# Attention with pooled keys plus a two-expert adapter on one core: the first batch's patch rows summed on two engines, and the second query group cast and transposed by DMA

## The chip, the cores and the metric

The kernel runs on one core of one Trainium2 chip. A core has five engines, each with its own instruction queue that is worked off strictly in order: TensorE (PE) multiplies matrices and, with an identity matrix, transposes them; VectorE (DVE) and ScalarE (ACT) do elementwise work; GpSimd (POOL) does elementwise work and issues the transfers that convert a type; SyncE (SP) issues transfers only. Sixteen DMA engines move the data. The metric is the device time of one execution in microseconds (us), smaller being better.

## The reference

For each of four batches there are 12288 queries of 128 numbers and an image of 384 x 32 positions of 128 numbers. The image is averaged over patches of 4 x 4, which leaves 768 rows, and multiplied by a matrix; the result serves as keys and values:

```python
kv_pool = kv.reshape(B, H // r, r, W // r, r, C).mean(axis=(2, 4))   # r = 4
kv_flat = kv_pool.reshape(B, -1, C) @ w_sr
s = scale * (q @ k.transpose(0, 2, 1))
a = np.exp(s); a /= a.sum(-1, keepdims=True) + 1e-09
x = a @ v
```

On x (49152 rows) stands a small mixture of adapters: logits = x @ w_gate for eight experts, the two best chosen, their softmax weights w, and out = x + sum of w * ((x @ A[e]) @ B[e]) with rank 16. All inputs and the output are float32.

## The kernel before

The 49152 queries are worked off in 96 chunks of 512, named k = 0 to 95; 24 chunks are one batch. Four chunks are a group of 2048 queries; group g holds chunks 4g to 4g + 3. A chunk goes through `scores` (six matrix products in three pairs, each pair into one of two PSUM buffers `sg`, each followed by one exponential on ACT into `em`), `attend` (24 matrix products into the single PSUM buffer `acc`, which also gives the row sums and the gate logits), `normalize` (DVE, `rinv` and `xn`; it frees `acc`), `top` and `route` (the choice of experts), `transposes`, `down`, `gate`, `up` and `finish` (the adapter). The loop over k from 4 to 95 staggers these steps over the chunks; every instruction is held in program order on its engine by `keep`, so what stands behind a waiting instruction waits with it.

**The prologue** makes what the loop needs: keys `kfT` and values `vx` of batch 0, and the scores of chunks 0 to 3. The image of batch 0 comes in three thirds h; a third has four patch rows r, and each row comes in two halves x, so SP issues 24 loads of 256 KB (`load_kv`, L98) in the order h, r, x. `prepare(0, nc.vector)` gives, for each third, the additions, then `keys(h)`, `keys2(h)` and `values(h)`. In the kernel before an addition (`pair_step`, L175) sums two of the four rows, rows 0 and 1 or rows 2 and 3, for one half: four additions on DVE for a third. `keys` then transposes on PE what is left, two row sums times two halves times four columns, which are 16 transposes of 128 x 128 float32 into one PSUM tile `kpT_ps`, where PE adds them up. The later batches are summed by POOL in the loop (L169, L171), from k = 10 on.

**The queries.** Matrix products need the queries transposed in bfloat16, `qT`. Groups 2 to 23 get there by two transfers: `cast_q(g)` (L79, issued by POOL) writes a bfloat16 copy of the group to a buffer in device memory, and `load_qT(g)` (L84, issued by SP) brings that copy in transposed. Groups 0 and 1 are loaded as float32 (`load_q`, L105) and turned by PE: `turn_q(g, m)` does four float32 transposes for chunk m of the group and a copy to bfloat16 on ACT (L116). Group 1's four loads stand behind the 24 image loads on SP; its four turns stand at the end of the prologue and in the steps k = 4, 5 and 6.

**The order around the change.** POOL's queue has nothing after the identity matrix but a one-element copy (`late`, L390), which waits for the last load of group 1 and so holds back the casts of groups 2 and 3 that stand behind it; the next entry is `route` of chunks 2 and 3. SP's queue has the image loads, group 1's loads, `b_f` and `a_f`, and then, in step k = 4, `load_qT(2)` and the first load of batch 1's image, one more of those in each of the next steps, and `load_qT(3)` at k = 8. PE's order at the seam is: scores of chunks 2 and 3 (last pair), the turn of chunk 4, `attend(0)`, then `scores(4, 0)`, and so on.

Of the kernel before, what the change touches and what calls it, by code (L numbers as in the profile page):

```python
# [15 lines left out]
ALU = mybir.AluOpType  # L16
# [4 lines left out]
def kernel(  # L21
# [10 lines left out]
    nc = tc.nc  # L32
# [7 lines left out]
    S = T // P  # L40
    GC = 4
# [35 lines left out]
    def cast_q(g):  # L77
        t = qdram.tile([GT, C], BF16, tag=f"q{g}", name=f"qbf{g}")
        keep(nc.gpsimd.dma_start(t, q[g // NG, (g % NG) * GT:(g % NG + 1) * GT]))  # L79
        q_bf[g] = t  # L80
# [20 lines left out]
    def load_q(g, lo, hi):  # L101
        if g not in q_f:
            q_f[g] = xpool.tile([P, GT // P, C], FP32, tag="xn", name="qf")
        src = q[0, g * GT:(g + 1) * GT].rearrange("(p j) c -> p j c", p=P)
        keep(nc.sync.dma_start(q_f[g][:, lo:hi], src[:, lo:hi]))  # L105

    def turn_q(g, m, engine):
        if m == 0:
            qT[g] = qpool.tile([P, GT], BF16, tag="qT", name="qT")
        ps = mtile([P, S, P], name="qT_ps")  # L110
        for i in range(S):
            mm(ps[:, i], q_f[g][:, m * S + i], id_f, is_transpose=True,
               start=(i == 0), stop=(i == S - 1))
        o = qT[g][:, m * T:(m + 1) * T].rearrange("p (s t) -> p s t", s=S)
        if engine is nc.scalar:
            keep(nc.scalar.copy(o, ps))  # L116
        else:
            keep(nc.vector.tensor_copy(o, ps))
# [7 lines left out]
    for h in range(3):  # L126
        for r in range(4):
            for x in range(2):
                load_kv(0, h, r, x)
    for m in range(GC):  # L130
        load_q(1, m * S, m * S + S)
    b_f = const.tile([P, C], FP32)
    keep(nc.sync.dma_start(b_f, moe_B.rearrange("e r c -> (e r) c")))
    a_f = const.tile([P, P], FP32)
# [23 lines left out]
    def prepare(b, adder):  # L158

        sums, rest = [], []  # L160

        def pool_step(h, step, lo, hi):
            t = kvr[b, h]
            if step < 3:
                u, v = t[:, 0].rearrange("p g c -> p (g c)"), t[:, step + 1].rearrange("p g c -> p (g c)")
            else:
                w = 2 * C if step == 3 else C
                u, v = t[:, 0, :, 0:w], t[:, 0, :, w:2 * w]
                keep(adder.tensor_tensor(u, u, v, op=ALU.add))  # L169
                return  # L170
            keep(adder.tensor_tensor(u[:, lo:hi], u[:, lo:hi], v[:, lo:hi], op=ALU.add))  # L171

        def pair_step(h, r, x):
            u, v = (kvr[b, h][:, r + i, x] for i in range(2))
            keep(adder.tensor_tensor(u, u, v, op=ALU.add))  # L175

        for h in range(3):
            if adder is nc.vector:
                sums.append([lambda h=h, r=r, x=x: pair_step(h, r, x)
                             for r in (0, 2) for x in range(2)])  # L180
                continue
            sums.append([lambda h=h, step=step, lo=lo: pool_step(h, step, lo, lo + 512)
                         for step in range(5) for lo in range(0, 1024 if step < 3 else 512, 512)])

        st = {}

        def keys(h):
            if h == 0:
                st["kpT"] = prep.tile([P, J, P], FP32, tag="kpT", name="kpT")
                kfT[b] = per_b.tile([P, J, P], BF16, tag="kfT", name="kfT")  # L190
            kpT = st["kpT"]
            ps = mtile([P, 2, P], name="kpT_ps")
            if adder is nc.vector:
                parts = [(r, i, c) for r in (0, 2) for i in range(2) for c in range(4)]
            else:
                parts = [(0, i, 0) for i in range(2)]
            for n, (r, i, c) in enumerate(parts):
                mm(ps[:, i], kvr[b, h][:, r, i, c * C:(c + 1) * C], id_f, is_transpose=True,
                   start=(n == 0), stop=(n == len(parts) - 1))
            keep(nc.vector.tensor_scalar(kpT[:, 2 * h:2 * h + 2], ps, 1.0 / 16.0, None,  # L200
                                         op0=ALU.mult))

        def keys2(h):
            kpT = st["kpT"]
            ps = mtile([P, 2, P], name="kfT_ps")
            mm(ps, w_sr_sb, kpT[:, 2 * h:2 * h + 2], start=True, stop=True)
            keep(nc.vector.tensor_copy(kfT[b][:, 2 * h:2 * h + 2], ps))

        def values(h):
            if h == 0:  # L210
                vx[b] = per_b.tile([P, J, VE], FP16, tag="vx", name="vx")
                keep(nc.vector.memset(vx[b][:, :, VC:VE], 1.0))
            ps = mtile([P, 2, VC], name="v_ps")
            for i in range(2):
                mm(ps[:, i], st["kpT"][:, 2 * h + i], wext, start=(i == 0), stop=(i == 1))
            keep(nc.vector.tensor_copy(vx[b][:, 2 * h:2 * h + 2, 0:VC], ps))
            if adder is not nc.vector:
                st["vb", h] = prep.tile([P, 2, C], BF16, tag="vb", name="vb")
                keep(nc.vector.tensor_copy(st["vb", h], ps[:, :, 0:C]))

        def turn(h):
            ps = mtile([P, 2, P], BF16, name="kfT_ps")
            for i in range(2):
                mm(ps[:, i], st["vb", h][:, i], id_bf, is_transpose=True,
                   start=(i == 0), stop=(i == 1))
            keep(nc.vector.tensor_copy(kfT[b][:, 2 * h:2 * h + 2], ps))

        for h in range(3):
            for f in (keys, keys2, values) if adder is nc.vector else (keys, values, turn):
                rest.append(lambda h=h, f=f: f(h))  # L230
        return sums, rest
# [155 lines left out]
    rest = []  # L387

    late = const.tile([P, 1], FP32)
    keep(nc.gpsimd.tensor_copy(late, q_f[1][:, GC * S - 1, 0:1]))  # L390
    for g in range(2, 4):
        cast_q(g)
    a_bf = const.tile([P, P], BF16)
    keep(nc.vector.tensor_scalar(a_bf, a_f, 0.5, None, op0=ALU.mult))
    b_bf = const.tile([P, C], BF16)
    keep(nc.vector.tensor_copy(b_bf, b_f))
    turn_q(1, 0, nc.scalar)


    att = {LA: [0], LA + 1: [1], LA + 2: [2, 3], LA + 3: [4, 5], LA + 4: [6, 7]}  # L400
# [16 lines left out]
    for k in range(LA, NCHUNK):  # L417
        b, i = divmod(k, NB)
        ka = att.get(k, [])
        kx = enter.get(k, [])  # L420
        if k % GC == 0:
            g = k // GC
            if 2 <= g + 1 < B * NG:
                load_qT(g + 1)
            if 4 <= g + 2 < B * NG and g + 2 not in q_bf:
                cast_q(g + 2)
        if b + 1 < B:
            if i == 4:
                sums, rest = prepare(b + 1, nc.gpsimd)
            if 4 <= i < 16:  # L430
                h, j = divmod(i - 4, 4)
                load_kv(b + 1, h, j, None)

        def after_norm(kn):
            top(kn)
            if kn == first[kn] + size[kn] - 1:
                route(first[kn])

        kn = [n for n in att.get(k - 1, []) if normed[n] == k]
        if k == LA:  # L440
            for s in range(S):
                attend(0, s)
            ka = []
        scores(k, 0)
        while later:
            later.pop(0)()
        for n in kn:
            normalize(n)
        pairs = [(kx[j] if j < len(kx) else None, kh[j] if j < len(kh) else None)
                 for j in range(max(len(kx), len(kh)))]  # L450
        for x_, h_ in pairs[:1]:
            transposes(x_, h_)
        if k + 1 in range(GC + 1, 2 * GC):
            turn_q(1, (k + 1) % GC, nc.scalar)
        scores(k, 1)
        for u_ in ku:
            up(u_)
            finish(u_)
        for a_ in ka[:-1]:
            for s in range(S):  # L460
                attend(a_, s)
            normalize(a_)
            after_norm(a_)
        if ka and len(ka) == 1:
            attend(ka[0], 0)
        for n in kn:
            after_norm(n)
        scores(k, 2)
        for x_ in kx[:1]:
            down(x_)  # L470
            gate(x_)
        if rest and i in (14, 15, 16, 18, 19, 20, 21, 22, 23):
            rest.pop(0)()
        for a_ in ka[-1:]:
            for s in range(1 if len(ka) == 1 else 0, S):
                attend(a_, s)
        for x_, h_ in pairs[1:]:
            transposes(x_, h_)
        for x_ in kx[1:]:
            down(x_)  # L480
            gate(x_)
        ku = kh
        kh = kx
        if b + 1 < B and 10 <= i < 21:
            h, j = divmod(i - 10, 4)
            for _ in range((4, 3, 1, 0)[j]):
                sums[h].pop(0)()
# [184 lines left out]
```

## Time and profile before

| what | value |
|---|---|
| median of three runs | 409.31 us (408.99 to 409.66) |
| the profiled execution's own time | 409.56 us |
| its span, first to last instruction | 407.6 us |
| PE busy | 379.6 us, 93% of the span |
| DVE, ACT, POOL busy | 324.5, 293.1, 170.7 us |
| mean granted TensorE clock | 0.991 |

The profile gives one execution. "Busy" counts an engine's instructions, and matrix products are pipelined, so a busy PE is not PE at its peak. A time such as 25.74 is in microseconds from the start of the span. In a row of the timeline the first number is the start, the second the duration, and `xN` says that N instructions of a kind were merged; a bracket at its end tells how long the engine sat idle before it and what ended that. For a transfer the row gives only its issue; the time to landing is in the answers for its line.

### The profile page before, as it was taken

To read this page: it belongs to the slowest core of one execution; us is meant where nothing else is said; L and a number is where in the kernel's file an instruction comes from. 1 tells how busy PE (TensorE), PEld (TensorE's weight loads), DVE (VectorE), ACT (ScalarE), POOL (GpSimd) and SP (SyncE) were. 2 spreads that over 40 slices of the span, in tenths; PEclk is the share of its full clock that TensorE was granted. 3 is DMA by queue.
4 is the path that set the end of the run, shared out by engine and by line. 5 is a ranking of instruction groups with operands and counts; after the bars stand their busy time and mean duration, and the time that the engine had idled before them with its cause. 6 is when DMAs were issued, how large, how long until landed. Compare 5 with 4: busy or idle time off the path is not lost.

```text
span 407.6 us, 11369 instructions
## 1 busy us (share of the span) xinstructions
PE 379.6 (93%) x4514; PEld 306.9 (75%) x4589; DVE 324.5 (80%) x948; ACT 293.1 (72%) x346; POOL 170.7 (42%) x289
## 2 busy tenths in 40 slices
PE   3798899999999999999999999999999999898992
PEld 2556778788888788888888788878888878677781
DVE  2553678888888888989888888988988888887873
ACT  2389468767678777867778877876777877665772
POOL 0010128888512319879411319879311322123342
PEclk9999999999999999999999999999999999999996
DMA  8998568984855999994855979996756548252213
GB/s 297 366 265 245 137 156 214 285 210 124 182 130 105 307 172 336 295 219 138 168 130 117 363 103 344 287 225 145 156 131 149 138 130 156 79 138 97 79 53 132
DMA packets 71319, 76.45 MB, mean 188 GB/s; under 512 B 49921, under 2 KB 50433, under 8 KB 70785
## 3 DMA queue, kind: packets, MB, share of 16 engines
q1 hardware_dynamic: 70128, 63.98, 53.8%
q0 software_dynamic: 704, 11.54, 16.7%
q8 instruction: 36, 0.59, 0.6%
q10 hardware_dynamic: 432, 0.20, 0.2%
q14 instruction: 19, 0.15, 0.1%
HBM read 50.53 MB, written 36.70 MB: 214 GB/s over the span
## 4 chain that ended last, share of the span: by engine, by line
PE 82%; DVE 7%; ACT 3%; DMA 3%; issue 2%; SPq 1%; POOL 1%; ACTq 0%; DVEq 0%; POOLq 0%
PE acc L68 34%; PE sg L68 23%; PE tt_ps L68 10%; PE h_ps L68 6%; PE d_ps L68 5%; ACT em L246 2%; DVE rinv L258 1%; DVE xn L263 1%; DMA kvr<-in_kv_dram 1%; SPq L98 1%; DMA w_sr_sb<-in_w_sr_dram 1%; PE kpT_ps L68 1%; DVE tts L333 1%; PE v_ps L68 1%; DVE hg L347 1%
## 5 line engine op out<-in xcount | busy, mean ns | idle before, releaser
L246 ACT ACTIVATE em<-sg 128x1024 f16<-128x1024 f32 x288 | 279.1, 1023 | 92.1 <-PE sg L68 59.5
L68 PE MATMUL acc<-vx,em 128*128 128x137 f16 x2280 | 171.7, 224 | 1.7 <-DVE xn L263 1.6
L68 PE MATMUL sg<-qT,kfT 128*128 128x512 bf16 x501 | 154.7, 378 | 2.7 <-ACT em L246 2.2
L68 PEld LDWEIGHTS <-em 128*128 128x128 f16 x2304 | 149.6, 98 | 4.0 <-DVE xn L263 2.2
L68 PEld LDWEIGHTS <-tts 128*128 128x128 bf16 x740 | 56.4, 98 | 45.8 <-DVE tts L333 2.1
L293 POOL TENSOR_TENSOR over<-xn,srt 128x128 f32<-128x128 f32 (+2 forms) x62 | 21.4, 365 | 157.0 <-DVE srt L281 157.0
L347 DVE TENSOR_TENSOR hg<-h_ps,gw 128x512 bf16<-128x512 f32 x93 | 64.2, 691 | 13.2 <-POOL gw L315 7.6
L263 DVE TENSOR_TENSOR xn<-acc,rinv 128x544 f32<-128x544 f32 x95 | 68.8, 725 | 3.3
L333 DVE COPY tts<-tt_ps 128x1024 bf16<-128x1024 bf16 (+1 forms) x96 | 64.4, 671 | 3.6 <-PE tt_ps L68 3.6
L171 POOL TENSOR_TENSOR kvr<-kvr 128x512 f32<-128x512 f32 x54 | 66.7, 1271 | 0.0
L360 DVE TENSOR_TENSOR osb<-d_ps,xn 128x512 f32<-128x512 f32 x91 | 62.6, 691 | 0.5 <-PE d_ps L68 0.5
L68 PEld LDWEIGHTS <-kfT 128*128 128x128 bf16 x576 | 45.9, 97 | 6.0 <-issue 3.7
L68 PEld LDWEIGHTS <-xn 128*128 128x128 bf16 x384 | 29.4, 98 | 22.0 <-ACT xn L585 0.5
L258 DVE RECIPROCAL rinv<-acc 128x4 f32<-128x4 f32 x95 | 17.3, 182 | 32.5 <-PE acc L68 31.4
L68 PE MATMUL h_ps<-a_bf,tts 128*128 128x128 bf16 x372 | 36.0, 219 | 2.8 <-DVE tts L333 1.6
L68 PE MATMUL tt_ps<-id_bf,xn 128*128 128x128 bf16 x372 | 35.9, 219 | 1.5
L68 PE MATMUL d_ps<-b_bf,tts 128*128 128x128 bf16 x364 | 35.2, 219 | 2.3 <-DVE tts L333 1.3
L68 PE MATMUL tt_ps<-id_bf,hg 128*128 128x128 bf16 x368 | 35.6, 219 | 0.3 <-DVE hg L347 0.3
L281 DVE MAX8 srt<-xn 128x8 f32<-128x8 f32 x380 | 34.3, 153 | 0.2
L314 POOL TENSOR_TENSOR gw<-th,over 128x128 f32<-128x128 f32 (+2 forms) x31 | 12.0, 389 | 39.2 <-ACT th L312 39.1
L68 PEld LDWEIGHTS <-hg 128*128 128x128 bf16 x384 | 25.5, 98 | 2.5 <-issue 1.1
L169 POOL TENSOR_TENSOR kvr<-kvr 128x512 f32<-128x512 f32 (+1 forms) x18 | 18.1, 1006 | 0.9
(77 smaller groups left out, 174.8 us busy)
## 6 DMA issues: line engine op xcount, KB each, us to landing
out_dram<-osb SPq DMA_DIRECT2D x95, 256.0 KB, 3.3
kvr<-in_kv_dram SPq DMA_DIRECT2D x36, 512.0 KB, 6.3
qbf<-in_q_dram POOLq DMA_DIRECT2D x22, 512.0 KB, 6.1
kvr<-in_kv_dram SPq DMA_DIRECT2D x24, 256.0 KB, 5.4
qf<-in_q_dram SPq DMA_DIRECT2D x1, 1024.0 KB, 5.1
qf<-in_q_dram SPq DMA_DIRECT2D x4, 256.0 KB, 5.2
qT<-qbf SPq DMA_TRANSPOSE x22, 6.3
out_dram<-osb ACTq DMA_DIRECT2D x1, 128.0 KB, 3.1
```

The costliest lines, as they stand in the source:

```text
L68: return keep(nc.tensor.matmul(*a, **k))
L169: keep(adder.tensor_tensor(u, u, v, op=ALU.add))
L171: keep(adder.tensor_tensor(u[:, lo:hi], u[:, lo:hi], v[:, lo:hi], op=ALU.add))
L246: keep(nc.scalar.activation(em[k][:, 2 * r:2 * r + 2], ps, AF.Exp, bias=0.0, scale=scale))
L258: keep(nc.vector.reciprocal(ri, acc[k][:, :, VC]))
L263: keep(nc.vector.tensor_tensor(x, acc[k][:, :, 0:VC], ri.unsqueeze(2).broadcast_to([P, S, VC]), op=ALU.mult))
L281: keep(nc.vector.max(srt[k0][:, m, s], xn[k][:, s, C:VC]))
L293: keep(eng.tensor_tensor(d, lg, so[:, :, i].unsqueeze(2).broadcast_to([P, n, 8]), op=ALU.subtract))
L314: keep(eng.tensor_tensor(w[:, 0:n], th, mask, op=ALU.mult))
L333: keep(nc.vector.tensor_copy(sb[:, lo:hi], ps[:, lo:hi]))
L347: keep(nc.vector.tensor_tensor(hg[k].rearrange("p s (e r) -> p (s e) r", e=E), hp[k].rearrange("p s (e r) -> p (s e) r", e=E), gw[k0][:, m ...
L360: keep(nc.vector.tensor_tensor(osb, dp[k], xn[k][:, :, 0:C], op=ALU.add))
```

## The change

The first part concerns the prologue's sums. For each third, rows 1, 2 and 3 are now added onto row 0, one after the other (`row_step`): the two additions of row 1 are done by POOL, the four of rows 2 and 3 by DVE. `keys` transposes only row 0's halves, eight transposes for a third in place of 16.

The second part concerns query group 1. Its four float32 loads, its four turns on PE and its four copies on ACT are gone. Group 1 is cast and brought in transposed as the later groups are: POOL casts groups 1, 2 and 3 one after the other, and SP issues `load_qT(1)` ahead of the loop. The one-element copy `late`, which the casts stand behind, now reads the last image load of batch 0.

```diff
-    for m in range(GC):
-        load_q(1, m * S, m * S + S)
...
-        def pair_step(h, r, x):
-            u, v = (kvr[b, h][:, r + i, x] for i in range(2))
-            keep(adder.tensor_tensor(u, u, v, op=ALU.add))
+        def row_step(h, r, x):
+            u, v = kvr[b, h][:, 0, x], kvr[b, h][:, r, x]
+            keep((nc.gpsimd if r == 1 else nc.vector).tensor_tensor(u, u, v, op=ALU.add))
...
-                sums.append([lambda h=h, r=r, x=x: pair_step(h, r, x)
-                             for r in (0, 2) for x in range(2)])
+                sums.append([lambda h=h, r=r, x=x: row_step(h, r, x)
+                             for r in (1, 2, 3) for x in range(2)])
...
-                parts = [(r, i, c) for r in (0, 2) for i in range(2) for c in range(4)]
+                parts = [(0, i, c) for i in range(2) for c in range(4)]
...
-    keep(nc.gpsimd.tensor_copy(late, q_f[1][:, GC * S - 1, 0:1]))
-    for g in range(2, 4):
+    keep(nc.gpsimd.tensor_copy(late, kvr[0, 2][:, 3, 1, 0:1]))
+    for g in range(1, 4):
         cast_q(g)
+        if g == 1:
+            load_qT(g)
...
-    turn_q(1, 0, nc.scalar)
...
-        if k + 1 in range(GC + 1, 2 * GC):
-            turn_q(1, (k + 1) % GC, nc.scalar)
```

## The prediction

> **What bounds the kernel now.** I read the page first, then the timeline of the first 62 us on all engines, then the answers for the lines of casts and transposing loads, and last the DMA queues in short stretches.
>
> ```profile
> PE 379.6 (93%) x4514; PEld 306.9 (75%) x4589; DVE 324.5 (80%) x948; ACT 293.1 (72%) x346; POOL 170.7 (42%) x289
> ...
> PE   3798899999999999999999999999999999898992
> ...
> PE 82%; DVE 7%; ACT 3%; DMA 3%; issue 2%; SPq 1%; POOL 1%; ACTq 0%; DVEq 0%; POOLq 0%
> ```
>
> A slice is 10.2 us. From the sixth on PE is nearly always busy, and 82% of the chain that ended last is PE. So from about 57 us on PE sets the pace, and what shifts PE's work before that shifts the end by the same amount. Both parts of the change lie before. This is the seam they touch, from the timeline:
>
> ```profile
> 23.24 0.42 PEld L68 LDWEIGHTS kpT_ps<-id_f,kvr 128*128 128x128 f32 x4 [0.18 <-DVE kvr L175]
> ...
> 25.74 0.19 POOL L390 COPY late<-qf 128x1 f32<-128x1 f32 x1 [24.44 <-DMA qf<-in_q_dram]
> 25.87 1.26 POOL L79 DMA_DIRECT2D qbf<-in_q_dram  x2
> ...
> 30.56 1.66 PE L68 MATMUL acc<-vx,em 128*128 128x137 f16 x24
> 31.33 0.63 ACT L116 CAST qT<-qT_ps 128x512 bf16<-128x512 f32 x1
> 31.36 2.52 SPq L84 DMA_TRANSPOSE qT<-qbf  x1
> ...
> 32.05 0.59 PE L68 MATMUL sg<-qT,kfT 128*128 128x512 bf16 x2
> ...
> 32.68 1.02 ACT L246 ACTIVATE em<-sg 128x1024 f16<-128x1024 f32 x1 [0.73 <-PE sg L68]
> ...
> 40.08 1.65 PE L68 MATMUL acc<-vx,em 128*128 128x137 f16 x24
> ```
>
> The reader is to see three times: chunk 4's first scores start at 32.05, right behind `attend(0)` (`acc` at 30.56); the two casts are issued at 25.87, once the last load of group 1 has landed; and the transposing load of group 2 is issued at 31.36, when its cast has landed. The third `acc` group, `attend(2)` at 40.08, is where I measure the shift.
>
> **Part one, the sums.** PE loses 24 of 48 transposes of `kpT_ps`. In the last third the weight loads of each four wait for a DVE addition (0.18 us in the row above); after the last addition four transposes remain, as now. So the saving is 0: the cover is DVE, whose additions per third stay four, 0.69 us each. POOL gets two per third, 1.26 to 1.28 us by L171's rows of the same shape. In the second third the image loads are issued 0.65 us apart and land 5.5 us later: row 1's halves at 14.7 and 15.3, the last half at 17.9. POOL adds until 16.0 and 17.25, so DVE's additions of the second half of row 2, then row 3, run from 17.3 to 19.25; before, the last ended at 18.7. That is 0.55 us late, and the last third follows with 0.55 us. `attend(0)` would start at 30.6, not 30.05 (where it could start once the turn ahead of it is gone). This costs 0 if chunk 4 waits for its queries beyond 32.2, and up to 0.55 us if not; that wait is the cover.
>
> No row of before shows POOL and DVE both adding float32 from SBUF; L171's additions run beside DVE work that reads at most one operand there. Bounds: side by side, as above; or in turns, 2 x 1.25 + 4 x 0.62 = 5.0 us a third, which is about 1 us late instead of 0.55, under the same cover. I take the first and keep the second.
>
> The Trainium skill speaks against this part: "SBUF — State Buffer", section Terms, says that GpSimd and VectorE take a shared port pair by an exclusive lock held for a whole instruction, the loser fully blocked. By that rule the sum takes the 1 us, still covered; no row here decides it.
>
> **Part two, the path of group 1's queries.** Removed: four SP issues (0.35 to 0.54 us each) and 1 MB of loads, which nothing waits for but `late`; four turns, 0.45 us of PE each; four copies on ACT, 0.47 us each in a row. Moved: `late` waits for the last image load, issued at 17.92 and landed 5.2 us later, at 23.1, and not for 25.69. Added: one cast, one transposing load, and PE's wait for that.
>
> 1. The first cast starts 0.18 us after that landing, as before: 23.28. Behind it on POOL stand the two other casts (0.5 to 0.76 us each), then nothing until 49.6.
> 2. The first cast before landed 5.5 us after its issue, and casts follow each other:
>
> ```profile
> L79 POOL DMA_DIRECT2D qbf<-in_q_dram x22: 512/579/755, 25.9 to 341.2; - x22
> ...
> DMA to landing us min/median/max: 5.4/6.1/8.9
> ```
>
> So `load_qT(1)` is issued at 23.28 + 5.47 + 0.02 = 28.77. The second cast landed 2.55 us after the first (31.34 and 33.89); its last packet left an engine at 33.48, 7.6 us after the first issue. A third adds 2.5 us: cast packets occupy the engines until 23.28 + 7.6 + 2.5 = 33.4.
> 3. The transposing load:
>
> ```profile
> L84 SPq DMA_TRANSPOSE qT<-qbf x22: 2289/3870/7020, 31.4 to 357.2; - x22
> ...
> DMA to landing us min/median/max: 4.7/6.3/9.5
> ```
>
> The first took 4.74 us. Its packets began at 32.96, when the engines had finished the second cast's, and it landed 2.6 us after the last cast packet. Do other packets get past a cast? The queues between 234.5 and 236.5, where a cast is in flight and a transposing load has just been issued:
>
> ```profile
> q0 software_dynamic: 3, 0.10, 29.5%
> q1 hardware_dynamic: 7, 0.02, 3.0%
> ...
> qT<-qbf SPq DMA_TRANSPOSE x1, 9.2
> ```
>
> In 2 us seven packets of the other queue start, and the load takes 9.2 us; its first packet starts at 239.0, as the last cast packet ends. A cast is 16 packets of 32 KB, one for each engine, 2.5 to 3.5 us each, and an engine takes nothing else meanwhile. After the change the third cast is queued on every engine before `load_qT(1)` is issued. Two ends: the load passes between the second and the third cast, 28.77 + 4.74 = 33.5; or it stands behind the third, 33.4 + 2.6 = 36.0. I take 36.0, by the 234 row.
>
> 4. PE's `scores(4, 0)` moves from 32.05 to 36.05, 4.0 us. Some comes back: from 32.68 on ACT was the pace (exponentials every 0.955 us, three copies of 0.47 us among them). Before, `attend(2)` followed the first exponential of chunk 4 by 7.4 us. After: four exponentials free the buffer for the third pair of chunk 5 (3.8), that pair (0.45), the rest of `attend(1)` (1.3), `rinv` and `xn` (1.0): 6.55 us, 0.85 less. Net: 4.0 - 0.85 = 3.15 us, and break-even where the queries land at 32.85.
>
> Behind `load_qT(1)` on SP wait `load_qT(2)`, four image loads of batch 1 and `load_qT(3)`. Pushed back some 3 us each they land near 39, 46 and 49; they are needed at 50.4 (chunk 8), 63.4 (POOL's first addition) and 65. The first output store, at 53.4, is behind them too. Cost 0, by 10 us of slack.
>
> Sum: 0 + 3.15 on the profiled execution's 409.56 gives 412.7; that execution is 0.25 above the median of the runs, which takes me to 412.5. The cases below are against that median, 409.31, too.
>
> One more cost has no row: PE would idle from about 32.1 to 36.05, and from 11 to 392 us its longest gap is 1.1 us at a granted clock of 1.00. Below, 0; above, half speed: PE's 4.1 us of work in chunks 4 and 5 (six pairs of 0.43 us, one `attend` of 1.5) doubled, against the 6.05 us that ACT's pace allows, 2.1 us more. I take 0, by the last stretch, where the clock stays at 0.99 between 396 and 400 with PE busy 2.36 of 4 us, and keep 2.1.
>
> The Trainium skill, "TensorE: Matmul & The Clock Gate", Part 1, says that an idle window of about 3.4 us halves PE's clock and that it takes as much sustained work to return; its windows run free, so a gap of 4 us may or may not hold one. By it the sum could be up to 2 us higher.
>
> **Rivals.**
> - B, the load passes the third cast. The queries land at 33.5 to 34.1, PE loses 0.7 to 1.2 us: 410.0 to 410.5. For it: the casts are separate packets with a gap between them; against: the next one started there within 0.02 us.
> - C, the held load plus one more loss (PE's clock, up to 2.1, or POOL's issue of the casts held up by DVE's additions until 25.0 (1.7)): up to 414.6. For it: the gap is new, and DVE adds from 21.9 to 24.9 without pause; against: no row shows either.
> - D, not slower: cast and transposing load are hidden. It decides at a landing of 32.85, which leaves 9.55 us from 23.28. The fastest cast and load of 22 each, 5.4 + 4.7, make 10.1. Landing by 32.1, where `attend(0)` ends with the later sums, gives 0.75 us back: 408.6.
>
> **How the numbers follow.** A measurement of this kernel can tell about 0.2% (0.8 us) from no change. A, as summed: 0.62; B: 0.17, a third of it within 0.2%; C: 0.14; D: 0.07, half of it faster by over 0.2%. Faster 0.03, same 0.10, slower 0.87. The range leaves out D, a little of B and the far end of C: 410.2 to 414.3.
>
> **What the profile will show.** Right: casts issued near 23.3, the transposing load's wait on SP ending near 28.8, PE idle before `sg` of chunk 4 until about 36 with the DMA as releaser, `attend(2)` near 43.2, the same rhythm after. Wrong: a landing near 33.5 (step 3), casts issued well after 23.3 (step 1), or a granted clock under 1 near 36 (the last cost).

## The result: 1.45% slower, nearly twice the loss that was forecast

The changed kernel takes 415.15 us (median of four runs, 414.99 to 415.64) against 409.28 us: a ratio of 1.0145, 95% interval 1.0127 to 1.0162. The direction was forecast; the time lies 2.65 us over the forecast and 0.85 us over the end of its range. The profiled execution took 415.29 us, with a span of 413.3 us.

The page of the changed kernel; as before, one slice is about 10.3 us, and PEclk gives the granted clock of PE in tenths:

```profile
PE   3784989999999999999999999999999999899992
...
PEclk9997999999999999999999999999999999999997
...
PE 82%; DMA 7%; DVE 4%; ACT 2%; SPq 1%; issue 1%; POOL 0%; DVEq 0%; ACTq 0%
```

PE still sets the pace from the sixth slice on. New are the dip in PE's row in the fourth slice, a clock of 0.7 in the same slice, and 7% of DMA in the chain where 3% stood before. Where that lies, the chain of the changed kernel shows in order of time (start, duration, what):

```profile
17.79 5.20 DMA kvr<-in_kv_dram
22.99 0.05 issue
23.04 0.12 POOL late L388
23.17 6.33 DMA qbf<-in_q_dram
29.50 0.02 issue
29.52 8.73 DMA qT<-qbf
38.25 0.05 issue
38.30 1.05 PE sg L68 x2
```

The last image load, the cast of group 1, its transposing load, and only then chunk 4's scores: three transfers in a row, the last two of them new on the chain. From the timeline of the changed kernel, with PE's wait in the bracket:

```profile
31.98 1.66 PE L68 MATMUL acc<-vx,em 128*128 128x137 f16 x24
...
38.30 1.89 PE L68 MATMUL sg<-qT,kfT 128*128 128x512 bf16 x4 [4.66 <-DMA qT<-qbf]
...
46.23 1.66 PE L68 MATMUL acc<-vx,em 128*128 128x137 f16 x24
```

Chunk 4's scores start at 38.30 and not 32.05, 6.25 us later; `attend(2)` starts at 46.23 and not 40.08, 6.15 us later. From there to the last chunk's exponentials the two traces stay 6.0 to 6.1 us apart, so the loss arises ahead of 47 us (the spans differ by 5.7 us; 0.3 us comes back behind those exponentials).

In stretches of the changed kernel (stretch, length, busy time of PE, weight loads, DVE, ACT and POOL, granted clock, DMA share, GB/s):

```profile
22.00:35.70 13.70, 9.70 (x66) 6.04 (x65) 7.16 (x23) 9.48 (x10) 2.20 (x5) 1.00 0.91 156
35.70:42.50 6.80, 3.82 (x8) 1.10 (x9) 0.09 (x1) 2.95 (x4) 0.00 (x0) 0.50 1.01 225
42.50:48.00 5.50, 5.43 (x62) 4.08 (x62) 1.69 (x6) 4.81 (x7) 0.00 (x0) 1.00 1.10 325
```

PE's clock is at half from 35.7 to 42.5; before, it was full throughout this time.

### The profile page after: what moved, and what is told of

Read it like the earlier page. It is cut to its first block, busy times and chain, and to the rows that moved or that the text cites. A ratio compares the mean times of both kernels' runs of the same rounds, so it can differ in the third digit from the quotient of the medians.

```text
span 413.3 us, 11370 instructions
## 1 busy us (share of the span) xinstructions
PE 383.7 (93%) x4549; PEld 304.4 (74%) x4549; DVE 325.4 (79%) x948; ACT 291.2 (70%) x342; POOL 178.4 (43%) x296
## 4 chain that ended last, share of the span: by engine, by line
PE 82%; DMA 7%; DVE 4%; ACT 2%; SPq 1%; issue 1%; POOL 0%; DVEq 0%; ACTq 0%
PE acc L68 34%; PE sg L68 28%; PE tt_ps L68 9%; PE h_ps L68 5%; PE d_ps L68 5%; DMA kvr<-in_kv_dram 3%; DMA qT<-qbf 2%; DMA qbf<-in_q_dram 2%; SPq L98 1%; DVE xn L261 1%; DMA w_sr_sb<-in_w_sr_dram 1%; PE v_ps L68 1%; DVE tts L331 1%; ACT em L244 1%; DVE hg L345 1%
## 5 line engine op out<-in xcount | busy, mean ns | idle before, releaser
L68 PE MATMUL sg<-qT,kfT 128*128 128x512 bf16 x576 | 173.7, 384 | 6.8 <-DMA qT<-qbf 4.7
L68 PE MATMUL tt_ps<-id_bf,hg 128*128 128x128 bf16 x368 | 35.6, 219 | 0.3 <-DVE hg L345 0.3
L312 POOL TENSOR_TENSOR gw<-th,over 128x128 f32<-128x128 f32 (+2 forms) x31 | 12.0, 387 | 38.9 <-ACT th L310 38.8
```

The costliest lines, as they stand in the source:

```text
L68: return keep(nc.tensor.matmul(*a, **k))
L312: keep(eng.tensor_tensor(w[:, 0:n], th, mask, op=ALU.mult))
```

## The experiments

**Is it the casts behind it that hold the load?** The casts of groups 2 and 3 wait on POOL, behind a one-element copy that reads group 1's transposed queries.

```diff
         if g == 1:
             load_qT(g)
+            late2 = const.tile([P, 1], BF16)
+            keep(nc.gpsimd.tensor_copy(late2, qT[1][:, GT - 1:GT]))
```

> The changed kernel, with the casts of groups 2 and 3 held on GpSimd until group 1's transposed queries have landed. Theory (the transposing load stands behind the third cast's 32 KB packets, and behind an instruction fetch on one DMA engine): with no cast behind the first, the queries land 4.7 to 5.3 us after the load's issue near 29, at 33.7 to 34.5 and not 38.25; PE's gap is under 1 us, its clock stays at 1.00 there, and the time is 410.0 to 411.0 us. Rival (the load is slow by itself, right behind the cast that wrote its source): landing still near 38, time near 415.

Measured: 411.16 us (ratio 1.0052, 1.0036 to 1.0069), 4.0 us less than the changed kernel. The answer for the transposing load of this run:

```profile
L84 SPq DMA_TRANSPOSE qT<-qbf x1: 2519/2519/2519, 28.8 to 28.8; - x1
...
DMA to landing us min/median/max: 4.7/4.7/4.7
```

4.7 us instead of 8.73; the queries land at 33.5. So the rival falls: the load isn't slow by itself, it stands behind the casts. The queues of the changed kernel from 30.5 to 32.4, with the load issued at 29.52, show the same from the other side; this is all that starts in these 1.9 us:

```profile
DMA packets 4, 0.07 MB, mean 34 GB/s; under 512 B 2, under 2 KB 2, under 8 KB 2
...
q0 software_dynamic: 4, 0.07, 17.7%
...
qT<-qbf SPq DMA_TRANSPOSE x1, 8.7
```

Not one packet of the load's queue (q1) is among them. The time is 0.16 us over what I expected. The profiled execution is the lowest of six (409.76 to 412.13), so its trace shows the landing, not the typical time. Two executions, at a mean granted clock of 0.992, took 409.76 and 410.07 us; the other four, at 0.977 to 0.986, took 411.03 to 412.13. There is no trace of those four, so whether the clock makes the difference is not shown, and what keeps this kernel 2.0 us above the kernel before stays open in part: the landing at 33.5, against the break-even at 32.85, accounts for 0.65.

**What does the half clock cost?** First in the changed kernel itself: PE gets work in its wait.

```diff
                 attend(0, s)
             ka = []
+            idle = mtile([P, T], name="idle_ps")
+            for _ in range(20):
+                mm(idle, kfT[0][:, 0], qT[0][:, 0:T], start=True, stop=True)
```

> The changed kernel, with 20 matrix products of 128 x 512, whose result nobody reads, on PE between the first chunk's attention and chunk 4's scores, about 4.3 us of work inside the 4.66 us that PE waits there. Theory (the wait lets PE's clock fall to half from 35.7 to 42.6, which costs 0.75 us of the 0.85 us that ACT should give back): the clock stays at 1.00, the queries land as before at about 38.2, and the time is 414.2 to 414.6 us. Rival (the clock's fall costs nothing, because ACT is the pace in that stretch): time 415.0 to 415.5.

Measured: 414.19 us (ratio 1.0123, 1.0108 to 1.0139), at the lower end of what the theory had, and the clock stays at 1.00 from 20.8 to 403 us. But in this run's trace the queries also land 0.9 us sooner, at 37.34, so it does not separate the two. A pair of runs does. The first takes the first part out (pairs on VectorE, 48 transposes) and holds the casts:

> Group 1 by DMA with the casts of groups 2 and 3 held until its queries have landed, and the patch rows summed in pairs by VectorE with 48 transposes, as in the kernel before. Theory (with the casts held, the queries land near 33.5; what the first part costs, 1.66 us alone, is then no longer covered, which is why holding the casts gave 411.16 and not 410): without the first part the loss is that of a landing at 33.5 against the break-even at 32.85, 0.7 us, so 409.6 to 410.4. Rival (the 2 us left are the DMA path's own): 410.8 to 411.5.

Measured: 412.74 us (1.0080, 1.0061 to 1.0099), well outside what I expected. The queries landed at 35.0 and not 33.5, and PE, whose prologue ends sooner without the first part, waited 3.0 us and lost its clock. The second adds 13 products in that wait, by the same edit as above:

> The run with held casts and sums in pairs, plus 13 matrix products of 128 x 512, whose result nobody reads, ahead of chunk 4's scores, 2.8 us of work in PE's gap from 32.0 to 35.0. Theory (that gap halves PE's clock from 34.0 to 40.8, which stretches the way from chunk 4's first scores to the third attention group from 7.2 to 8.5 us): the clock stays at 1.00, that way takes 7.2 us, and the time falls from 412.74 by 1.0 to 1.5, to 411.2 to 411.7 us. Rival (ACT is the pace in that stretch, and the clock costs nothing): 412.4 to 413.0.

Measured: 411.44 us (1.0059, 1.0040 to 1.0078), 1.30 us less (1.1 us if each is set against the runs of the kernel before that were taken with it), with the load landing at 35.0 in both. The stretch after the wait, first in the run without the 13 products:

```profile
34.10:40.80 6.70, 5.31 (x16) 2.04 (x17) 0.07 (x1) 4.33 (x5) 1.10 (x3) 0.50 0.89 168
```

and in the run with them:

```profile
34.10:40.80 6.70, 4.78 (x33) 2.41 (x33) 0.23 (x2) 5.09 (x7) 1.09 (x3) 1.00 0.88 171
```

From chunk 4's first scores to `attend(2)` it took 8.54 us at half clock and 7.21 us at full clock. The wait's clock is thus shown to cost 1.3 us here. In the changed kernel the same way took 7.93 us, which puts it at 0.7 us there. What is left of the second run, 2.15 us, is the landing: 35.0 against the break-even at 32.85.

**What does the first part cost alone, and why?**

```diff
-            u, v = (kvr[b, h][:, r + i, x] for i in range(2))
-            keep(adder.tensor_tensor(u, u, v, op=ALU.add))
+            u, v = kvr[b, h][:, 0, x], kvr[b, h][:, r, x]
+            keep((nc.gpsimd if r == 1 else nc.vector).tensor_tensor(u, u, v, op=ALU.add))
```

(with the eight transposes and the order of the changed kernel; group 1 loaded and turned by PE as before)

> The kernel before with the first part alone: patch rows summed by GpSimd and VectorE, 24 transposes in place of 48; query group 1 loaded and turned by PE as before. Prediction's step: the additions are 0.55 us late, or 1.0 us where VectorE and GpSimd take turns, no cover here: 409.8 to 410.3. Theory from the changed kernel's trace (PE, with less to do in the prologue, gets its full clock at 22.1 us and not at 10.8, and a VectorE addition took 1.74 us beside a GpSimd one): the first chunk's attention starts 1.4 to 1.9 us later, time 410.7 to 411.2. Rival (fewer transposes help): under 409.0.

Measured: 410.83 us (1.0038, 1.0023 to 1.0053), 1.66 us over the kernel before. Then the same with work for PE where it waits for the additions:

```diff
+            if adder is nc.vector:
+                idle = mtile([P, P], name="idle_ps")
+                for _ in range(8):
+                    mm(idle, id_f, id_f, is_transpose=True, start=True, stop=True)
             for n, (r, i, c) in enumerate(parts):
```

> The first part alone, with eight transposes of the identity matrix, whose result nobody reads, put ahead of each third's eight transposes on PE, where PE waits for the additions. Theory (of the 1.7 us that the first part costs alone, PE's half clock from 14.3 to 21.2 us is the larger share): the clock stays at 1.00 from about 11 us on and the time falls from 410.83 to 409.6 to 410.1 us; what is left is the later additions, 0.5 to 0.9 us. Rival (the additions, VectorE held up beside GpSimd, cost all of it): 410.6 to 411.2.

Measured: 409.89 us (1.0018, 1.0009 to 1.0027). The stretch from 14.3 to 21.1 us of the run without the added work, and then of the run with it:

```profile
14.30:21.10 6.80, 5.58 (x17) 2.81 (x18) 3.94 (x6) 1.94 (x2) 3.70 (x4) 0.50 1.03 379
```

```profile
14.30:21.10 6.80, 4.84 (x27) 2.95 (x28) 4.46 (x7) 2.53 (x3) 3.95 (x4) 1.00 1.05 402
```

The transposes that the first part saves had kept PE's clock up. Of 1.66 us, 0.94 go with the clock; the other 0.7 are put down to the later additions. The two traces place only a part of this: `attend(0)` starts at 31.60 and, with the added work, at 31.20 (30.56 before), which is 0.40 us for the clock and 0.64 us for the additions. Why these are late is in the answers for the additions' line of the changed kernel, on DVE and then on POOL (min, median, max in ns):

```profile
L173 DVE TENSOR_TENSOR kvr<-kvr x12: 677/680/1740, 9.7 to 25.6; 128x512 f32<-128x512 f32 x12
...
  POOL kvr L173: 2.0, 1
```

```profile
L173 POOL TENSOR_TENSOR kvr<-kvr x6: 1257/1264/1271, 8.4 to 21.1; 128x512 f32<-128x512 f32 x6
```

The DVE addition of 1740 ns starts at 9.72 while POOL adds from 9.65 to 10.92, and it ends 0.54 us after that one. The first part alone has two such, of 1703 and 1372 ns, and each of them, too, ends 0.55 us after the POOL addition beside it. In the run with the added work the second third has one of 1742 ns (from 15.78 us): that third's last addition ends at 19.33 and not 18.69, the last third's at 25.04 and not 24.40, 0.64 us late like `attend(0)`. DVE waits for POOL, as the Trainium skill has it ("SBUF — State Buffer", Terms).

**Does the second part alone explain the whole?** The kernel before with the second part only:

> The kernel before with the second part alone: query group 1 cast and transposed by DMA; patch rows summed in pairs by VectorE, 48 transposes on PE. Theory (the wait for the queries decides and covers the first part): the queries land at 36.5 to 38.3, time 413.5 to 415.3. Rival (the first part costs its 1.4 us on top): 411.5 to 413.5.

Measured: 415.24 us (1.0149, 1.0134 to 1.0164). It equals the changed kernel. So behind the wait for the queries the first part costs nothing on balance, as forecast, and nothing is gained by it. The two traces are not alike, though: without the first part the queries landed at 37.67, 0.58 us sooner, but PE waited 6.3 us, was at half clock from 33.4 to 43.6, and took 8.60 us from chunk 4's scores to `attend(2)` where the changed kernel took 7.93. In these two the differences nearly cancel.

**Why was the landing at 38.25?** The changed kernel once more, for a second trace:

> The changed kernel once more, for a second profile of it. Theory of the landing at 38.25 (15 of the load's 16 completions at 36.7, the last behind an instruction fetch on its DMA engine): cast issues near 23.2, most completions near 36 to 37, and a last one that is 1 us or more later only where an instruction fetch or a late cast stands on its engine. Rival (the last completion is always late): the same 1.5 us without a fetch near it. Time 415.0 to 415.6.

Measured: 416.88 us in a single run, 1.3 us over the range I gave, with the queries landing at 39.02. Here all 16 completions are late (15 of them from 38.9 to 39.0), not one, so the theory as I wrote it fits the first trace only. What this trace shows is a stop in the middle of the load. The queues from 34.6 to 38.0, in 40 slices of 0.085 us:

```profile
GB/s 18 105 205 289 289 289 476 271 271 271 274 256 27 18 15 0 0 0 0 0 6 9 9 9 9 9 12 9 9 130 289 289 289 289 292 342 271 271 280 289
...
q8 instruction: 1, 0.02, 2.1%
```

For 1.4 us, from 35.6 to 37.0, nearly nothing moves on any engine, and the one transfer besides is a 16 KB instruction fetch from 35.16 to 36.33. In the first trace such a fetch lies from 36.01 to 37.18, with 15 completions at 36.6 to 36.7 and the last at 38.25. Between the last cast packet and the landing lie 3.8 and 4.5 us in these two traces and 3.8 in the run with 20 products, all three with a 16 KB fetch in that time. It is 2.6 us in the kernel before, with no fetch; 3.0 with the first part alone, where a 16 KB fetch ends 0.25 us into that time; and 3.1 with the second part alone, where a fetch of 8 KB lies in it (36.08 to 36.49). That the fetch is the cause is argued from these six traces; I did not move a fetch to try it.

**Do the traces point to a faster kernel?** Two places in the kernel before have an engine that waits beside one that is the pace. In the last third DVE's four additions start late; and ACT copies group 1's turned queries while it is the pace and DVE idles.

```diff
-            keep(adder.tensor_tensor(u, u, v, op=ALU.add))
+            eng = nc.gpsimd if (h, r) == (2, 0) else adder
+            keep(eng.tensor_tensor(u, u, v, op=ALU.add))
```

> The kernel before with one edit: in the last third GpSimd sums rows 0 and 1, in pairs as before, and VectorE only rows 2 and 3; the 48 transposes on PE stay. Theory (before, VectorE's four additions of the last third start at 21.9 us, behind other work, and end 0.6 us after the last image load could have let them): the last addition ends at 23.8 and not at 24.4, everything up to the first chunk's attention moves 0.5 to 0.6 us ahead, time 408.5 to 408.8. Rival (the queue of exponentials on ACT takes the gain): 409.0 to 409.3.

Measured: 408.33 us (0.9981, 0.9972 to 0.9990), 0.17 us under what I expected. The last addition ends 0.78 us after the last image load's landing, where it ended 1.3 us after it before. In this trace `attend(2)` starts at 39.76, 0.32 us sooner than before, so the theory places less than half of the 0.83 us gained.

```diff
-    turn_q(1, 0, nc.scalar)
+    turn_q(1, 0, nc.vector)
...
-            turn_q(1, (k + 1) % GC, nc.scalar)
+            turn_q(1, (k + 1) % GC, nc.vector)
```

> The kernel before with one edit: the four copies of group 1's turned queries are made by VectorE and not by ACT. Theory (from 32.7 to 41 us ACT is the pace, with three of these copies among its exponentials, while VectorE idles 4 us): the third group of attention products starts 0.8 to 1.4 us sooner, time 407.8 to 408.5. Rival (VectorE's chain from normalization to routing is the pace there): 409.0 to 409.4.

Measured: 407.89 us (0.9970, 0.9959 to 0.9982), the fastest of all. ACT and PE in this run:

```profile
32.23 4.69 ACT L246 ACTIVATE em<-sg 128x1024 f16<-128x1024 f32 x5 [1.21 <-PE sg L68]
...
39.13 1.65 PE L68 MATMUL acc<-vx,em 128*128 128x137 f16 x24
```

Five exponentials now run in a row, with no copy among them. From `attend(0)` to `attend(2)` it takes 9.0 us instead of 9.5; the rest of the 1.27 us this trace does not place (its image loads landed 0.5 us sooner).

> The two edits together: GpSimd sums rows 0 and 1 of the last third, VectorE makes the four copies of group 1's queries. If both theories hold and add up, 407.2 to 408.0 us; if one of them takes the other's gain, 408.2 to 408.7.

Measured: 408.20 us (0.9973, 0.9964 to 0.9983). In time the two do not add up. In the traces they do, up to the last two exponentials, which start at 390.43 before and at 389.97, 389.49 and 389.00 in the three runs; why the times do not follow is not shown. The intervals of the three overlap, so which is the best of them is not settled.

## Why the prediction was wrong

**What bounds, and part one: right.** PE sets the pace behind the seam, the transposes saved gain nothing, and the wait for the queries covers what the first part costs: the second part alone gives the same time as both. Without that cover the forecast's 0.55 to 1.0 us was too little; it is 1.66 us, because the step looked for the saved transposes' worth only in PE's time and not in PE's clock (0.94 us).

**Steps 1 and 3, the mechanism: right.** The casts were issued at 23.17 (forecast 23.28), the load stood behind the third cast and not between the casts, and with the casts held its time to landing is 4.7 us, as step 3 had it from the row before. The first cast took 6.33 us to land and not 5.47, which cost nothing while the load had the third cast to wait for.

**Steps 2 and 3, the size: wrong by 2.25 us.** The landing was set at 36.0 and came at 38.25. Two terms were too small. Step 2 let the cast packets end at 33.4; the last ended at 34.45, because one of the 16 cast packets of each round ended 0.9, 1.0 and 1.3 us behind the next-latest one (0.3 us in both rounds of the trace before). What makes that packet late is not shown. Step 3 let the load land 2.6 us after that; it took 3.8, for which the instruction fetch is argued and not shown. Both numbers were read from one instance in the trace before, as if they were fixed.

**The last cost, PE's clock: wrong by 0.75 us.** It was named and bounded (0 to 2.1 us), and set at 0 by a stretch where PE was busy in short bursts. That was a misreading. The answer from which the stretch was taken has one more row, and in it the clock is at half (kernel before):

```profile
396.00:400.00 4.00, 2.36 (x24) 1.51 (x25) 2.57 (x6) 2.62 (x8) 1.73 (x3) 0.99 0.02 4
400.00:407.60 7.60, 1.38 (x10) 0.98 (x10) 1.45 (x3) 1.48 (x4) 1.26 (x1) 0.50 0.47 175
```

The way from chunk 4's scores to `attend(2)` took 7.93 us and not the 7.18 of step 4; at full clock 7.21 us is what three runs show. So of the 0.85 us that ACT should give back, 0.10 came.

With these, the sum closes at `attend(2)`: 3.15 forecast, 2.25 for the landing, 0.75 for the clock make 6.15, the shift measured there. Rival C had the right form (the held load and a further loss) but held the landing at 36.0, and its other candidate, casts issued late because of DVE's additions, did not come (23.17); A and C with both terms at their measured size give the result.

## What to carry to other kernels

A transfer that must land before the loop can go on is priced by what is queued ahead of it on the DMA engines, not by its own time to landing: two casts that nobody needed soon cost 4 us here, and holding them back gave that back, though the kernel stayed 2.0 us over the one before. A term read from a single instance deserves the spread of its kind (this line's loads had 4.7 to 9.5 us). Work taken off TensorE in a stage where it waits anyway saves nothing and can cost its clock.

## What the runs showed of the hardware that I had not expected

- PE's clock fell to half 2.0 to 2.1 us into the wait in four traces (waits of 3.0, 4.7, 6.3 and 6.7 us) and stayed there for 6.8 us in two of them and 10.2 us in the other two. "TensorE: Matmul & The Clock Gate", Part 1, in the Trainium skill asks for an idle window of about 3.4 us; a wait of 3.0 us was enough here.
- PE also lost its clock in the prologue of the run with the first part alone, from 14.3 to 21.1 us, with no wait over 1.8 us; eight idle transposes more a third brought it back. In all five traces with eight transposes a third the half clock ends only at 20.8 to 22.4 us; in none of the seven with sixteen is there a half clock from 13.6 us to the end of the prologue. In two of the five (the changed kernel's first trace and the run with the casts held) the profile records no clock before 22 us and prints 1.00; there the products tell it, two score products taking 1.06 us at 20.79 and 0.59 us at 22.31 in the changed kernel.
- An addition on DVE with both operands in SBUF took up to 1742 ns beside one on POOL, 680 alone. The other way round, POOL's one-element copy took 0.45 to 0.70 us beside DVE's additions (0.70, 0.45 and 0.46 in the three runs with group 1 by DMA and sums in pairs, 0.66 in the changed kernel's second trace), 0.18 alone, and the casts behind it started later by the difference.
